# A gated mix of two attention layers: first phase and lead rearranged

## The chip, the cores and the metric

The kernel runs on one core of one Trainium2 chip. The core has five engines that work side by side, each through its own list of instructions in order: TensorE (PE; its weight loads are shown as PEld), VectorE (DVE), ScalarE (ACT), GpSimd (POOL) and SyncE (SP). An instruction waits on semaphores for the work it needs. Transfers between the core's memory (SBUF) and the device memory are issued from the lists of SP, ACT or POOL and carried out by 16 DMA engines. TensorE writes its results to PSUM, eight banks of 128 x 512 numbers, which ACT and DVE read.

The metric is the device time of one execution in microseconds (us), lower is better. The kernel before was run three times, and one execution was taken with the hardware profiler.

## The reference

Two attention layers with 32 heads of 18 dimensions work on the same input of 2048 rows by 576 columns, and a gate per row mixes their outputs. Layer A has its own keys and values per head; in layer B all heads share one key and one value. All is in 32-bit floating point.

```python
def reference(A_x, A_wqkv, A_wo, B_x, B_wq, B_wk, B_wv, B_wo, gate_w):
    ...
        qkv = (lambda x, *d: x.transpose(*d))((x @ wqkv).reshape(B, S, 3, H, Dh), 2, 0, 3, 1, 4)
        q, k, v = qkv[0], qkv[1], qkv[2]
        scale = Dh ** -0.5
        scores = jnp.einsum("bhqd,bhkd->bhqk", q, k) * scale
        p = _softmax(scores, axis=-1)
        o = jnp.einsum("bhqk,bhkd->bhqd", p, v)
        return (lambda x, *d: x.transpose(*d))(o, 0, 2, 1, 3).reshape(B, S, D) @ wo
    ...
        q = (lambda x, *d: x.transpose(*d))((x @ wq).reshape(B, S, H, Dh), 0, 2, 1, 3)
        k = x @ wk
        v = x @ wv
        scores = jnp.einsum("bhqd,bkd->bhqk", q, k) * (Dh ** -0.5)
    ...
    x = A_x
    g = _sigmoid((x * gate_w).sum(-1, keepdims=True))
    a = _A_ref(x, A_wqkv, A_wo)
    b = _B_ref(x, B_wq, B_wk, B_wv, B_wo)
    return g * a + (1 - g) * b
```

## The kernel before

The order of all engines' work is written out by hand: what stands first in the Python text stands first in each engine's list. TensorE multiplies in a reduced 32-bit format, so every operand of a product is kept as a high part and a low part (`h` and `l`, the remainder), and a product is the sum of high by high, high by low and low by high.

**First phase (L197 to L262).** The weights of all queries, shared key, shared value, gate and per-head keys lie side by side in `wall`, 14 row tiles of 128 columns (`MT`). `load5` (L120) brings five blocks of 128 contraction rows of a weight tile or an X tile with three transfers: one for four blocks and two for the last 64 rows, which are stored twice so that the fifth block carries both a high and a low part. X comes in eight tiles of 256 columns. `split_x` (L206) makes high and low parts of X: a copy on ACT, a subtract on DVE (L211) and a correction on DVE for the doubled rows (L212). `prep_w` (L134) does the same for a weight tile. `project(mt, c, w)` (L142) multiplies row tile `mt` by a chunk of 512 columns of X: 14 matmuls into one bank of the PSUM pool `ps` (three banks), then a copy of the high part by ACT (L150), the low part by DVE (L156), and a store of each: the high part from ACT's list into `qk_d[0]`, the low part from POOL's into `qk_d[1]`. Ten of the row tiles hold keys; there a difference of two chunks is stored in the same way (`kd_d`). Row tiles 0 and 1 are done together chunk by chunk while X arrives, the other twelve after that, four chunks each: 56 tiles of work in all. For chunk after chunk of row tile 0 the shared value is transposed by four small matmuls (`shared_v`, L174). At L236 to L240 and L253 the rows of the shared key and of the first three heads' queries are loaded back from the stored projections, from POOL's list. They are transfers of 18 rows of 2048 numbers; each goes twice into SBUF, to partitions from 0 (`SB`) and from 64 (`MB`).

Transfers are counted by sixteen semaphores in two rings of eight, one ring for SP and ACT together and one for POOL; a transfer is issued only when the one eight places before it in its ring has landed.

**Lead (T below 0 in the loop at L628).** Softmax needs the largest score of each row of a head before the exponentials. The step of maxima, `step_max(u, i, c)` (L329), multiplies 128 queries by 512 keys into a bank of the pool `pm` (four banks), and DVE takes the row maximum (L350). It runs `LEAD` = 22 steps of four banks ahead of the main loop. Before the loop proper, eleven rounds of two steps each (88 banks) are done as `LEADS` says, with `V` units between: `project_v` (L184), 32 units of 14 matmuls each that make layer A's values from X and are copied out by ACT (L190). `max_rows` (L352) sends a finished head's maxima through a small transfer into two extra rows of its queries.

**Main loop.** 512 rounds of two steps. A round has eight score matmuls (`s`, L376, into `ps`), each followed by an exponential on ACT (L383), the products with the values (`P`, `h`, `H`, L390), eight banks of maxima for later steps (`m`, and `x` with L344 and L347, which spare DVE one bank), and from some round on the output projection. In round T = 0 (`FIRST`) there are no products yet, and its eight banks of maxima stand between the scores.

Of the kernel before, what the change touches and what calls it, by code (L numbers as in the profile page):

```python
# [29 lines left out]
PROJ = [("h", "h", k, 128) for k in range(NKT)] + [("h", "l", k, 128) for k in range(NKT - 1)] + \  # L30
       [("l", "h", k, 128) for k in range(NKT)]
# [11 lines left out]
def gated_mix_kernel(ctx: ExitStack, tc: tile.TileContext, xT, wall, wv, wo, out):  # L43
# [15 lines left out]
    qk_d = [dram.tile([MT * P, S], F32, name=f"qk{x}") for x in "hl"]  # L59
    kd_d = [dram.tile([MT * P, 512], F32, name=f"kd{x}") for x in "hl"]  # L60
# [23 lines left out]
    dma(ones_r.rearrange("a (b c) -> (a b) c", c=32), ones)  # L84
# [5 lines left out]
    def load_rows(t, r, parts, eng=None):  # L90
        for b in (MB, SB):
            for i, y in enumerate(parts):
                dma(t[b + 18 * i:b + 18 * i + 18, :], qk_d[y][r:r + 18, :], eng)

    def load_q(u, eng=None):
        load_rows(qs[u % 3], q_row(u), (0, 0, 1), eng)

    def load_kd(t, r, eng=None):
        for i, y in enumerate((0, 1, 0)):
            dma(t[MB + 18 * i:MB + 18 * i + 18, :], kd_d[y][r:r + 18, :], eng)  # L100

    def load_k(t, r, eng=None):
        load_rows(t, r, (0, 1, 0), eng)
# [25 lines left out]
    def load_w(mt):  # L129
        st = wpool.tile([P, NKT, P], F32, name="wst", bufs=6)  # L130
        load5(st, wall[mt])
        return st

    def prep_w(st):  # L134
        w = {y: wpool.tile([P, NKT, P], F32R, name=f"w{y}") for y in "hl"}
        split_w(st, w, nc.vector)
        return w
# [4 lines left out]
    def project(mt, c, w):  # L142

        fp = ps_s.tile([P, 512], F32, name="ps")
        cs = slice(c * 512, (c + 1) * 512)
        for n, (a, b, k, kr) in enumerate(PROJ):
            nc.tensor.matmul(fp, w[a][:kr, k, :], X[b][:kr, k, cs], start=(n == 0), stop=(n == len(PROJ) - 1))  # L147
        h = stp.tile([P, 512], F32R, name="ph")
        l = stp.tile([P, 512], F32R, name="pl")
        nc.scalar.activation(h, fp, AF.Copy)  # L150
        if mt == 0 or c == 0 and mt in HAS_K:
            st = stp.tile([P, 512], F32, name="pst", bufs=3)
            nc.scalar.activation(st, fp, AF.Copy)
            if c == 0:
                KD[mt] = st
        nc.vector.tensor_tensor(l, fp, h.bitcast(F32), op=OP.subtract)  # L156
        if c == 1 and mt in HAS_K:
            d = stp.tile([P, 512], F32, name="pd", bufs=1)
            nc.vector.tensor_tensor(d, fp, KD.pop(mt), op=OP.subtract)
            dh, dl = (stp.tile([P, 512], F32R, name=f"pd{y}", bufs=1) for y in "hl")  # L160
            split(d, dh, dl, nc.scalar, nc.vector)
        dma(qk_d[0][mt * P:(mt + 1) * P, cs], h, nc.scalar)
        dma(qk_d[1][mt * P:(mt + 1) * P, cs], l, nc.gpsimd)
        if c == 1 and mt in HAS_K:
            dma(kd_d[0][mt * P:(mt + 1) * P, :], dh, nc.scalar)
            dma(kd_d[1][mt * P:(mt + 1) * P, :], dl, nc.gpsimd)
        if mt == 0:
            dma(z_d[cs], st[ROW_G:ROW_G + 1, :], nc.scalar)
            return c, st
# [11 lines left out]
    for t in vst:  # L181
        nc.gpsimd.memset(t, 1.0)
# [13 lines left out]

    WV = []  # L197
    with tc.tile_pool(name="xs", bufs=6, side="right") as xsp:
        W = [load_w(0)]
        XS = []  # L200

        def load_x(c):
            XS.append(xsp.tile([P, NKT, 256], F32, name="xs"))
            load5(XS[c], xT[:, 256 * c:256 * c + 256])

        def split_x(c):  # L206
            xs = XS[c]
            cs = slice(c * 256, (c + 1) * 256)
            xh = X["h"][:, :, cs]
            nc.scalar.activation(xh, xs, AF.Copy)  # L210
            nc.vector.tensor_tensor(X["l"][:, :, cs], xs[:, 0:4], xh[:, 0:4].bitcast(F32), op=OP.subtract)  # L211
            nc.vector.tensor_tensor(xh[64:128, 4], xs[64:128, 4], xh[64:128, 4].bitcast(F32), op=OP.subtract)  # L212

        for c in range(4):
            load_x(c)
        W.append(load_w(1))
        for c in range(4, 8):
            load_x(c)
        for mt in range(2, 6):
            W.append(load_w(mt))  # L220
        WP = [prep_w(W.pop(0))]
        for c in range(2):
            split_x(c)
# [9 lines left out]
    VS = [vwp.tile([P, NKT, 288], F32, name="vwst"), None]  # L233
    load5(VS[0], wv[:, 0:288])

    for b in (SB, MB):  # L236
        dma(ksb[b + 54:b + 56, :], ones_r, nc.gpsimd)
    load_k(ksb, ROW_KB, nc.gpsimd)
    load_kd(kdb, ROW_KB, nc.gpsimd)
    load_q(0, nc.gpsimd)  # L240

    def project_rest():
        WN = prep_w(W.pop(0))
        for mt in range(2, MT):
# [3 lines left out]
            if mt + 4 < MT:  # L248
                W.append(load_w(mt + 4))
            for c in range(4):  # L250
                project(mt, c, w)
            if mt in (4, 5):
                load_q(mt - 3, nc.gpsimd)  # L253
            if mt in (8, 11):
# [3 lines left out]
                if hf == 0:  # L258
                    VS[1] = vwp.tile([P, NKT, 288], F32, name="vwst")
                    load5(VS[1], wv[:, 288:576])  # L260

    project_rest()  # L262
# [66 lines left out]
    def step_max(u, i, c, low=False):  # L329
# [10 lines left out]
        pm = ps_m.tile([P, 512], F32, name="pm")  # L340
# [286 lines left out]
    LEADS = "V.A mA0 MA1 mA2 MA3 V.B mB0 MB1 mB2 MB3"  # L627
    for T in range(-LEAD, NSTEP + 2, 2):  # L628
        if T == 0:
            open_ph2()  # L630
# [3 lines left out]
        if M >= 16 and M % 16 == 0 and M // 16 - 1 < NU:  # L634
# [3 lines left out]
        for op in (LEADS if T < 0 else FIRST if T == 0 else ALONE if alone else UNIT if units else PLAIN).split():  # L638
            k, second, c = op[0], op[1:2] == "B", op[2:]
            if k == "V":  # L640
                while len(vunits) > 32 * (-T - 1 - (c == "B")) // LEAD:
                    project_v(*vunits[0], WV[vunits[0][1]])
                    vunits.pop(0)
            elif k == "x":
                if M + 2 < NSTEP:
                    step_max(*divmod(M + 2, 16), "x")
            elif k in "mM":
                step_max(*divmod(M + second, 16), int(c), k == "M")
# [56 lines left out]
```

## Time and profile before

| | us |
|---|---|
| runs of the kernel before | 2789.89, 2790.0, 2787.21 |
| median | 2789.89 |
| the profiled execution, its own time | 2789.11 |
| its span, first to last instruction | 2787.2 |
| TensorE busy | 2758.0 (99%) |
| VectorE busy | 2419.9 (87%) |
| ScalarE busy | 2433.3 (87%) |
| GpSimd busy | 211.9 (8%) |
| bytes moved | 214.53 MB, mean 77 GB/s |
| granted TensorE clock, mean | 0.997 |

Times in the rows below are from the start of the span. A row of the table of stretches gives, for each engine, its busy time and the number of its instructions, then the granted TensorE clock as a share of full speed, the mean busy share of the DMA engines and the bytes they moved a second. A row of the timeline gives start and duration, engine, line, operation, what it writes and reads, how often it came in a row, and in brackets how long the engine was idle before and what ended that. In a list of groups, the count is followed by the busy time, the mean of one in ns and the idle time before them. The chain that ended last is followed backwards from the last instruction, at each step to whatever released it. Instructions of one engine overlap a little, so a busy share of 100% does not say that the engine could not go faster. In a line that ends with three durations and a slash, these are the shortest, the median and the longest in ns, followed by the first and the last start.

### The profile page before, as it was taken

How to read it: one execution, taken by the hardware profiler on the slowest of the kernel's cores; microseconds unless marked ns; L12 is line 12 of the kernel's file. 1: busy time of each engine (PE TensorE's matmuls, PEld its weight loads, DVE VectorE, ACT ScalarE, POOL GpSimd, SP SyncE). 2: the span in 40 equal slices, each digit the busy share in tenths (PEclk: the TensorE clock that was granted, in tenths of full speed). 3: DMA queues.
4: the chain of work that ended last, by engine and by line, in shares of the span. 5: the costliest groups of instructions: out<-in, count | busy, mean ns of one | idle time of the engine just before them, and what ended most of it. 6: DMA issues, size and time to landing. Idle time of an engine off the chain costs nothing.

```text
span 2787.2 us, 57590 instructions
## 1 busy us (share of the span) xinstructions
PE 2758.0 (99%) x22132; PEld 1226.1 (44%) x22132; DVE 2419.9 (87%) x4495; ACT 2433.3 (87%) x4775; POOL 211.9 (8%) x368
## 2 busy tenths in 40 slices
PE   7999999999999999999999999999999999999998
PEld 5888433333333333333333444444434443334554
DVE  3346999999999999999999999999999999998873
ACT  3231899999999999999999999999999999998776
POOL 2220000001001100100110001000100010011000
PEclk9999999999999999999999999999999999999999
DMA  8662011111112111211143224222332223234412
GB/s 252 228 231 76 27 33 33 31 46 53 40 26 57 56 32 31 65 41 33 45 100 106 64 70 108 68 75 75 87 89 76 67 81 84 65 77 118 109 35 86
DMA packets 136738, 214.53 MB, mean 77 GB/s; under 512 B 55302, under 2 KB 94166, under 8 KB 124777
## 3 DMA queue, kind: packets, MB, share of 16 engines
q1 hardware_dynamic: 115751, 167.56, 23.0%
q10 hardware_dynamic: 14120, 22.30, 2.2%
q0 software_dynamic: 6592, 20.99, 2.2%
q8 instruction: 174, 2.85, 0.4%
q14 instruction: 101, 0.83, 0.1%
HBM read 137.23 MB, written 64.77 MB: 72 GB/s over the span
## 4 chain that ended last, share of the span: by engine, by line
PE 97%; DMA 2%; DVE 1%; SPq 0%; issue 0%; ACT 0%; POOL 0%; POOLq 0%; DVEq 0%
PE ps L376 41%; PE acc L390 38%; PE ps L147 5%; PE pm L341 5%; PE pm L516 4%; PE ps L187 2%; DMA qkl<-pl 0%; DMA ksb<-qkh 0%; DMA xs<-xT 0%; DMA wst<-wall 0%; SPq L49 0%; DVE mx L350 0%; PE pm L376 0%; DMA qkh<-ph 0%; DVE oacc L528 0%
## 5 line engine op out<-in xcount | busy, mean ns | idle before, releaser
L383 ACT ACTIVATE pt<-ps 128x512 f32<-128x512 f32 x4052 | 2127.4, 611 | 106.6 <-PE pm L341 42.8
L350 DVE TENSOR_REDUCE mx<-pm 128x1 f32<-128x512 f32 x3096 | 1976.3, 684 | 163.4 <-PE pm L341 121.3
L376 PE MATMUL ps<-qs,ksb 56*128 56x512 f32 x2688 | 907.9, 437 | 0.0
L341 PE MATMUL pm<-ksb,qs 54*128 54x512 f32 x2364 | 825.1, 445 | 0.9 <-DVE mx L350 0.3
L376 PEld LDWEIGHTS ps<-qs,ksb 56*128 56x128 f32 x2688 | 437.6, 184 | 683.9 <-ACT pt L383 660.4
L390 PE MATMUL acc<-pt,vb 128*19 128x256 f32 (+1 forms) x6144 | 592.4, 457 | 0.1
L390 PE MATMUL acc<-pt,vg 128*19 128x256 f32 (+1 forms) x5656 | 579.4, 481 | 0.4 <-DVE oe L402 0.4
L376 PE MATMUL ps<-qs,ksa 56*128 56x512 f32 x1364 | 456.3, 437 | 0.0
L341 PE MATMUL pm<-ksa,qs 54*128 54x512 f32 x1232 | 433.4, 443 | 0.0
L341 PEld LDWEIGHTS pm<-ksb,qs 54*128 54x128 f32 x2364 | 379.6, 184 | 10.5 <-DVE mx L350 4.0
L376 PEld LDWEIGHTS ps<-qs,ksa 56*128 56x128 f32 x1364 | 218.5, 184 | 343.9 <-ACT pt L383 317.0
L347 DVE CUSTOM_DVE_ANT_0 junk<-pm,xb 128x512 bf16<-128x512 f32 x500 | 340.1, 680 | 0.0
L344 ACT ACTIVATE xb<-pm 128x512 f32<-128x512 f32 x500 | 304.1, 608 | 0.0
L341 PEld LDWEIGHTS pm<-ksa,qs 54*128 54x128 f32 x1232 | 200.4, 184 | 0.9
L390 PEld LDWEIGHTS acc<-pt,vb 128*19 128x19 f32 x6144 | 104.2, 97 | 209.9 <-issue 199.6
L390 PEld LDWEIGHTS acc<-pt,vg 128*19 128x19 f32 x5656 | 96.5, 97 | 208.2 <-issue 195.4
L341 PE MATMUL pm<-kdb,qs 54*128 54x512 f32 x372 | 148.9, 400 | 0.0
L116 POOL CAST mh<-mt 128x32 fp32r<-128x32 f32 x64 | 13.5, 210 | 1712.2 <-DVE mt L358 1712.2
L156 DVE TENSOR_TENSOR pl<-ps,ph 128x512 fp32r<-128x512 f32 x56 | 38.5, 691 | 97.2 <-ACT ph L150 69.4
L150 ACT ACTIVATE ph<-ps 128x512 fp32r<-128x512 f32 x56 | 33.5, 597 | 101.6 <-PE ps L147 89.3
L147 PE MATMUL ps<-xh,wh 128*128 128x512 f32 x280 | 76.6, 405 | 19.2 <-ACT xh L210 13.1
L147 PE MATMUL ps<-xh,wl 128*128 128x512 f32 x280 | 72.7, 389 | 0.0
(103 smaller groups left out, 1316.4 us busy)
## 6 DMA issues: line engine op xcount, KB each, us to landing
qs<-qkh SPq DMA_DIRECT2D x244, 144.0 KB
qs<-qkl SPq DMA_DIRECT2D x122, 144.0 KB
qkh<-ph ACTq DMA_DIRECT2D x56, 256.0 KB
qkl<-pl POOLq DMA_DIRECT2D x56, 256.0 KB, 3.1
ksa<-qkh SPq DMA_DIRECT2D x88, 144.0 KB
onh<-oh SPq DMA_DIRECT2D x32, 256.0 KB
onl<-ol SPq DMA_DIRECT2D x32, 256.0 KB
oih<-onh SPq DMA_DIRECT2D x16, 512.0 KB
```

The source lines that it names most:

```text
L147: nc.tensor.matmul(fp, w[a][:kr, k, :], X[b][:kr, k, cs], start=(n == 0), stop=(n == len(PROJ) - 1))
L150: nc.scalar.activation(h, fp, AF.Copy)
L156: nc.vector.tensor_tensor(l, fp, h.bitcast(F32), op=OP.subtract)
L187: nc.tensor.matmul(fp[:, 0:288], X[b][:kr, k, st_ * P:(st_ + 1) * P], w[a][:kr, k, :], start=(n == 0), stop=(n == len(PROJ) - 1))
L341: nc.tensor.matmul(pm, qs[u % 3][b:b + 54, i * P:(i + 1) * P], k, start=True, stop=True)
L344: nc.scalar.activation(MX["x", u, i], pm, AF.Relu)
L347: nc.vector.tensor_tensor_reduce(junk, pm, MX.pop(("x", u, i)), 1.0, -3e38, op0=OP.add, op1=OP.max, accum_out=MX[u][:, i, c:c + 1])
L350: nc.vector.tensor_reduce(MX[u][:, i, c:c + 1], pm, axis=AX.X, op=OP.max)
L376: nc.tensor.matmul(ps, kst(u)[b:b + 56, i * P:(i + 1) * P], qs[u % 3][b:b + 56, c * 512:(c + 1) * 512], start=True, stop=True)
L383: nc.scalar.activation(pt, ps, AF.Exp, scale=SCALE)
L390: nc.tensor.matmul(acc[32 * j:32 * j + 19, a:b], v_of(u, i), PT[u, i, j][:, a:b], start=(i == 0), stop=(i == 15), skip_group_check=True)
L516: nc.tensor.matmul(fp[:, 0:288], o[b][:r, t, s2 * P:(s2 + 1) * P], w[a][:r, t, 288 * hf:288 * hf + 288], start=(n == 0), stop=(n == 3 * nt ...
```

## The change

It has several parts.

- The order of products in a tile (`PROJ`) puts the two of the fifth block last.
- The two DRAM tensors for high and low parts become one of twice the size, and `project` keeps both parts in one SBUF tile `phl` (four buffers instead of three and three) and stores them with one transfer from POOL's list; the same for `kd`. ACT issues no transfers in the first phase.
- `load5` takes four neighbouring rows to a partition instead of rows 128 apart; X comes as two tiles of 256 columns and three of 512. The 64-row rests of the first five tiles are issued from POOL. Three weight tiles come ahead of the later X tiles, and three row tiles are worked on per chunk. The very first tile is done in two halves of 256 columns.
- Six matmuls of constants run on TensorE before the first data. A copy of a constant is put at the head of ACT's list, and the store of that constant goes behind the loads.
- The row loads are collected and issued from SP's list, one after each tile of `project_rest`.
- The lead is written as 16 visits of two V units and six banks; of these, two banks go to the pool `ps` and four to `pm`. It does 24 steps, so round T = 0 has no maxima but `x`.

```diff
-PROJ = [("h", "h", k, 128) for k in range(NKT)] + [("h", "l", k, 128) for k in range(NKT - 1)] + \
-       [("l", "h", k, 128) for k in range(NKT)]
+PROJ = [(a, b, k, 128) for a, b in (("h", "h"), ("l", "h"), ("h", "l")) for k in range(NKT - 1)] + \
+       [("h", "h", NKT - 1, 128), ("l", "h", NKT - 1, 128)]
...
-    dma(ones_r.rearrange("a (b c) -> (a b) c", c=32), ones)
+    nc.scalar.activation(ones, ones, AF.Copy)
...
-    def load5(t, src):
-        dma(t[:, 0:4, :], src[0:512, :].rearrange("(k p) m -> p k m", p=P))
-        dma(t[0:64, 4, :], src[512:576, :])
-        dma(t[64:128, 4, :], src[512:576, :])
+    def load5(t, src, rest=None):
+        dma(t[:, 0:4, :], src[0:512, :].rearrange("(p k) m -> p k m", p=P))
+        dma(t[0:64, 4, :], src[512:576, :], rest)
+        dma(t[64:128, 4, :], src[512:576, :], rest)
...
-    def project(mt, c, w):
+    def project(mt, c, w, parts=1):
...
+        g = 512 // parts
+        for i in range(parts):
+            for n, (a, b, k, kr) in enumerate(PROJ):
+                nc.tensor.matmul(fp[:, g * i:g * i + g], w[a][:kr, k, :],
+                                 X[b][:kr, k, c * 512 + g * i:c * 512 + g * i + g],
+                                 start=(n == 0), stop=(n == len(PROJ) - 1))
+        hl = stp.tile([P, 2, 512], F32R, name="phl", bufs=4)
+        nc.scalar.activation(hl[:, 0, :], fp, AF.Copy)
...
+        nc.vector.tensor_tensor(hl[:, 1, :], fp, hl[:, 0, :].bitcast(F32), op=OP.subtract)
+        dma(qk_d[:, mt * P:(mt + 1) * P, cs].rearrange("a p f -> p a f"), hl, nc.gpsimd)
...
-        dma(qk_d[0][mt * P:(mt + 1) * P, cs], h, nc.scalar)
-        dma(qk_d[1][mt * P:(mt + 1) * P, cs], l, nc.gpsimd)
...
+    def later(o, i):
+        rows_back.append(lambda: dma(o, i))
+
+    def bring_row():
+        if rows_back:
+            rows_back.pop(0)()
...
+            XS.append(xsp.tile([P, NKT, 256 if half else 512], F32, name="xsh" if half else "xs", bufs=2))
+            load5(XS[c], xT[:, 256 * c:256 * c + 256] if half else xT[:, 512 * (c - 1):512 * c], rest)
...
+        W = [load_w(0, nc.gpsimd)]
+        load_x(0, nc.gpsimd)
+        load_x(1, nc.gpsimd)
+
+        warm = ps_m.tile([P, 512], F32, name="pm")
+        for i in range(6):
+            nc.tensor.matmul(warm[:, 0:304], ident, vb.rearrange("p k d -> p (k d)"), start=True, stop=True)
+        W.append(load_w(1, nc.gpsimd))
+        W.append(load_w(2, nc.gpsimd))
+        for c in range(2, 5):
             load_x(c)
+        dma(ones_r.rearrange("a (b c) -> (a b) c", c=32), ones)
+        for mt in range(3, 6):
             W.append(load_w(mt))
...
         for c in range(4):
+            keep = project(0, c, WP[0], 2 if c == 0 else 1)
+            if c == 3:
+                WN = prep_w(W.pop(0))
+            project(1, c, WP[1])
             if c < 3:
                 split_x(2 * c + 2)
                 split_x(2 * c + 3)
-            keep = project(0, c, WP[0])
-            project(1, c, WP[1])
             shared_v(*keep)
+            project(2, c, WP[2])
...
-    load_k(ksb, ROW_KB, nc.gpsimd)
-    load_kd(kdb, ROW_KB, nc.gpsimd)
-    load_q(0, nc.gpsimd)
+    load_k(ksb, ROW_KB, put=later)
+    load_kd(kdb, ROW_KB, put=later)
+    for u in range(3):
+        load_q(u, put=later)
...
             for c in range(4):
                 project(mt, c, w)
-            if mt in (4, 5):
-                load_q(mt - 3, nc.gpsimd)
+                bring_row()
...
+    banks = [(M, c) for M in range(LEAD + 2) for c in range(4)]
+    for v in range(16):
+        if v == 11:
+            max_rows(0)
+        for st_, hf in vunits[2 * v:2 * v + 2]:
+            project_v(st_, hf, WV[hf])
+        for n, (M, c) in enumerate(banks[6 * v:6 * v + 6]):
+            step_max(*divmod(M, 16), c, c % 2 == 1, ps_s if n < 2 else ps_m)
...
-    FIRST = "sA0 mA2 sA1 mA0 sA2 mA3 mA1 sA3 mB0 sB0 mB1 sB1 mB2 sB2 mB3 sB3 x"
+    FIRST = "sA0 sA1 sA2 sA3 sB0 sB1 sB2 sB3 x"
...
-    LEADS = "V.A mA0 MA1 mA2 MA3 V.B mB0 MB1 mB2 MB3"
-    for T in range(-LEAD, NSTEP + 2, 2):
+    for T in range(0, NSTEP + 2, 2):
```

More of the change, by code (lines that the diff above doesn't have):

```diff
@@ L56, in gated_mix_kernel @@
     ctx.enter_context(tc.manual_schedule())
-    qk_d = [dram.tile([MT * P, S], F32, name=f"qk{x}") for x in "hl"]
-    kd_d = [dram.tile([MT * P, 512], F32, name=f"kd{x}") for x in "hl"]
+    qk_d = dram.tile([2, MT * P, S], F32, name="qk")
+    kd_d = dram.tile([2, MT * P, 512], F32, name="kd")
     m_d = [dram.tile([P, 64], F32, name=f"m_d{i}") for i in range(4)]
@@ L127, in split_w, with load_w @@
         eng_l.tensor_tensor(w["l"], st, w["h"].bitcast(F32), op=OP.subtract)
-    def load_w(mt):
+    def load_w(mt, rest=None):
         st = wpool.tile([P, NKT, P], F32, name="wst", bufs=6)
-        load5(st, wall[mt])
+        load5(st, wall[mt], rest)
         return st
     def prep_w(st):
-        w = {y: wpool.tile([P, NKT, P], F32R, name=f"w{y}") for y in "hl"}
+        w = {y: wpool.tile([P, NKT, P], F32R, name=f"w{y}", bufs=3) for y in "hl"}
         split_w(st, w, nc.vector)
@@ L327, in gated_mix_kernel, with step_max @@
     MX = {}
-    def step_max(u, i, c, low=False):
+    def step_max(u, i, c, low=False, pool=ps_m):
         if u not in MX:
@@ L339, in step_max @@
             k = kst(u)[b:b + 54, c * 512:(c + 1) * 512]
-        pm = ps_m.tile([P, 512], F32, name="pm")
+        pm = pool.tile([P, 512], F32, name="pm" if pool is ps_m else "ps")
         nc.tensor.matmul(pm, qs[u % 3][b:b + 54, i * P:(i + 1) * P], k, start=True, stop=True)
```

104 lines of the change are left out of this document (47 added, 57 removed).

## The prediction, made before the changed kernel ran

> **What bounds the kernel now.** I read the engines' busy time by stage first, with edges where the work changes: the first matmul, the last long wait of the projections, the first gated V unit, the first score of the main loop, its second and third round.
>
> ```profile
> core 0: us, PE busy (x) PEld busy (x) DVE busy (x) ACT busy (x) POOL busy (x), PEclk, DMA share, GB/s
> 0.00:13.11 13.11, 0.00 (x0) 0.00 (x1) 3.33 (x7) 4.56 (x4) 1.57 (x9) 1.00 0.60 183
> 13.11:71.64 58.53, 50.80 (x212) 39.76 (x212) 23.91 (x36) 20.70 (x29) 15.24 (x29) 0.97 0.91 266
> 71.64:206.45 134.81, 134.81 (x587) 111.42 (x588) 52.32 (x73) 43.86 (x70) 34.60 (x65) 0.99 0.65 229
> 206.45:285.96 79.51, 79.51 (x538) 68.82 (x537) 53.47 (x89) 14.11 (x35) 1.93 (x11) 1.00 0.24 81
> 285.96:295.89 9.93, 8.98 (x33) 2.92 (x30) 9.07 (x16) 6.86 (x12) 0.00 (x0) 0.72 0.07 24
> 295.89:301.45 5.56, 5.56 (x44) 2.21 (x41) 4.27 (x8) 4.62 (x9) 0.00 (x0) 0.89 0.00 0
> ```
>
> TensorE sets the pace nearly everywhere. It stands still for 13.1 us at the start and for 58.53 - 50.80 = 7.7 us more up to 71.64; the first round of the loop (9.93 us) is the other weak place. The rounds from the second on keep their instructions in their order, so the change lives or dies in these 301 us.
>
> Next the longest pieces of the chain that ended last, which name the stalls and give the price of a tile (14 matmuls), and one group of the list of lines.
>
> ```profile
> 7.69 6.07 DMA xs<-xT
> 51.46 10.87 DMA ksb<-qkh
> 63.58 7.22 DMA qkl<-pl
> 71.64 135.20 PE ps L147 x588
> ...
> L174 PE MATMUL pm<-ident,pst 18*128 18x18 f32 x16 | 1.7, 215 | 1.6 <-ACT pst L153 1.6
> ```
>
> 135.20 / 588 = 0.230 us a matmul, 3.22 us a tile. The other 56 x 14 - 588 = 196 matmuls, 14 tiles, are done by 71.64. They need 45.1 us, and the 16 small transposes beside them 1.7, so the front loses 71.64 - 46.8 = 24.9 us: 13.1 before the first matmul, 7.7 idle, 4.1 in slow matmuls. That is the reserve of the first phase. The timeline shows where it goes.
>
> ```profile
> 1.01 0.29 POOL masks.py:199 TENSOR_SCALAR_AFFINE_SELECT ident<-ident 128x128 f32<-128x128 f32 x1
> 1.84 0.35 SPq L49 DMA_DIRECT2D ones_r<-ones  x1
> 2.24 1.74 SPq L49 DMA_DIRECT2D wst<-wall  x3
> 4.03 7.43 SPq L49 DMA_DIRECT2D xs<-xT  x12
> 5.85 1.28 ACT L126 ACT_TABLE_LOAD   x1 [5.85 <-DMA wst<-wall]
> 8.98 1.27 ACT L210 ACTIVATE xh<-xs 128x1280 fp32r<-128x1280 f32 x1 [1.10 <-DMA xs<-xT]
> 10.28 1.23 DVE L211 TENSOR_TENSOR xl<-xs,xh 128x1024 fp32r<-128x1024 f32 x1 [1.54 <-ACT xh L210]
> 11.54 0.42 DVE L212 TENSOR_TENSOR xh<-xs,xh 64x256 fp32r<-64x256 f32 x1
> 13.11 2.51 PE L147 MATMUL ps<-xh,wh 128*128 128x512 f32 x5 [13.11 <-ACT xh L210]
> 15.42 1.91 PE L147 MATMUL ps<-xl,wh 128*128 128x512 f32 x4
> 17.12 1.35 PE L147 MATMUL ps<-xh,wl 128*128 128x512 f32 x5
> 48.38 2.50 PE L147 MATMUL ps<-xh,wh 128*128 128x512 f32 x5 [3.37 <-ACT wh L126]
> 70.90 0.69 DVE L156 TENSOR_TENSOR pl<-ps,ph 128x512 fp32r<-128x512 f32 x1 [9.96 <-DMA qkl<-pl]
> ```
>
> Loads leave SP one by one (7.43 / 12 = 0.62 us each) behind a store that waits for DVE. The first tile needs two X tiles, and its first nine matmuls run at half speed (2.51 us for 5, later 1.35). At 70.90 DVE has waited 9.96 us for a store buffer, since the stores of the low part stand on POOL's queue behind the row loads of L237 to L240, and these in turn wait for other DMAs.
>
> **The change part by part.**
>
> *Start.* The constant's store leaves SP's head, so w0, X0, X1 can go from about 0.9, each as one issue; their 64-row rests go from POOL after 1.30.
>
> ```profile
> L49 POOL DMA_DIRECT2D qkl<-pl x56 | 30.6, 546 | 133.8 <-DVE pl L156 128.6 <-DMA wst<-wall 2.2 <-DVE vb L177 2.2
> qkl<-pl POOLq DMA_DIRECT2D x56, 256.0 KB, 3.1
> ```
>
> At 0.55 us an issue, X0's second rest (the fourth) leaves at 3.5. From issue to landing it takes between 1.9 us (before, w0: 3.98 to 5.85) and the median 3.1, so X0 is there at 5.4 to 6.6. The activation table is loaded meanwhile, by the copy on ones. Splitting X0 takes 1.27, and the two-part tile starts on 256 columns: first matmul at 6.7 to 7.9, taken 7.5. Its first hl product waits for xl (1.23 after xh), its k=4 pair for the correction (0.42); the second half's come another 1.65 later, so tile 0 ends near 11.1, 0.4 over its 3.22.
>
> *Idle matmuls.* They cost nothing by themselves: PE has no data until 7.5.
>
> ```profile
> 2763.79 1.19 PE L543 MATMUL pm<-vb,ident 128*128 128x304 f32 x4
> ```
>
> The same instruction starts every (1.19 - 0.42) / 3 = 0.26 us at full speed, 0.52 at half; six last 1.5 to 3.1 us from about 1.9 and end by 5, with 2.5 us of idle time behind. The slow start cost 2.51 + 1.91 - 9 x 0.23 = 2.3 us before. Nothing in this trace shows such a short burst; I take half of it, 1.0, bounds 0 and 2.3. The Trainium skill ("TensorE: Matmul & The Clock Gate", Part 1: The HAM clock gate) has full speed come after about 3.4 us of sustained matmuls and go after an idle window as long; the row agrees (slow from 13.11 to about 17.1, slow again after 3.37 us idle). By it, six idle matmuls fall just short, and this term would be 2.3, the sum below 1.3 smaller.
>
> *X and weights in order of need.* Three tiles a chunk ask 9.7 us of PE for 1.31 MB of X and 1.57 MB of stores.
>
> ```profile
> 10.00:20.00 10.00, 6.73 (x20) 4.91 (x21) 4.34 (x6) 3.67 (x5) 0.00 (x0) 1.00 1.00 283
> 30.00:40.00 10.00, 8.35 (x40) 6.48 (x39) 5.93 (x9) 4.80 (x7) 1.20 (x3) 1.00 0.92 303
> ```
>
> At 0.29 MB/us the second chunk (3.6 MB, with w0 to w2) lands near 16 and is split by 20; PE is through three tiles and transposes at 18.4. The third (6.5 MB with stores) lands near 25.5 for a split due at 25, the fourth has waited for the second's buffer and lands near 34 for one due at 35. PE and DMA are nearly even, so stalls are small but certain. Pieces of wall grow to 2 KB; I give no credit for it.
>
> *Stores and rows.* ACT sheds 70 issues; POOL issues 66 stores of 512 KB where it had 66 of 256 KB and 29 row loads. An issue costs between 0.55 (as now) and 1.09 (two of them): either hides under 3.22 a tile. Four buffers instead of three allow a store about 4 x 3.22 - 1.3 = 11.6 us before ACT's copy (0.6) or DVE's subtract (0.7) waits, and then, two tiles on, PE. The rows now stand on SP; behind a row that waits stand only weight loads, needed three row tiles (39 us) later. But SP runs ahead: some 15 rows follow within 45 to 60 us, together with stores. For late X and crowded stores I take 3.0 us of PE time, bounds 0 and 11 (the 7.22 and 3.37 us waits of before coming back). The transposes keep their 1.6 of idle time.
>
> Front after: 7.5 + 0.4 + 1.0 + 3.0 + 1.6 = 13.5 us lost, against 24.9. Gain 11.4; bounds 24.9 - (6.7 + 0.4 + 0 + 0 + 1.6) = 16.2 and 24.9 - (7.9 + 0.4 + 2.3 + 11 + 1.6) = 1.7. It shifts all that follows.
>
> *Lead.*
>
> ```profile
> 275.94 0.69 PEld L187 LDWEIGHTS ps<-vwh,xh 128*128 128x128 f32 x5 [0.25 <-ACT vst L190]
> 277.89 0.82 PE L187 MATMUL ps<-vwh,xh 128*128 128x288 f32 x5
> 279.82 0.73 PE L341 MATMUL pm<-ksb,qs 54*128 54x512 f32 x4
> 280.49 0.93 PE L187 MATMUL ps<-vwh,xh 128*128 128x288 f32 x5
> 282.55 0.84 PE L341 MATMUL pm<-ksb,qs 54*128 54x512 f32 x4
> 283.08 2.48 DVE L350 TENSOR_REDUCE mx<-pm 128x1 f32<-128x512 f32 x4 [0.24 <-PE pm L341]
> 283.32 0.93 PE L187 MATMUL ps<-vwh,xh 128*128 128x288 f32 x5
> ```
>
> Two V units take 279.82 - 275.94 = 3.88 us, four banks 0.67 (two by two on the halves of the array); where banks return after one unit, DVE (2.48 for four) isn't through and they cost 0.77. A visit of two units and six banks: 3.88 + 1.5 x 0.67 = 4.89; DVE needs 6 x 0.62 = 3.7 of it, and a bank's buffer (four of pm, one or two of ps) is written again only a visit later. Sixteen visits: 78.2 against 79.5, gain 1.3, with 8 banks more done. Bounds: 0.67 again for all six, 74.5, gain 5.0; or each visit 0.3 longer by waits for ps, which V units and banks now share, 83.0, loss 3.5.
>
> *First round.*
>
> ```profile
> L344 ACT ACTIVATE xb<-pm x41: 603/605/622, 313.7 to 498.8; 128x512 f32<-128x512 f32 x41
> 285.90 7.86 DVE L350 TENSOR_REDUCE mx<-pm 128x1 f32<-128x512 f32 x13 [0.33 <-PE pm L341]
> 290.00:295.89 5.89, 5.71 (x21) 1.81 (x19) 5.03 (x10) 4.07 (x8) 0.00 (x0) 0.52 0.01 3
> ```
>
> A steady round takes (498.8 - 313.7) / 40 = 4.63 us. Before, the first two take 9.93 + 5.56 = 15.5: DVE works off 13 banks, and the clock falls to 0.52. Without banks the first is ACT's nine instructions: 2 x 4.63 = 9.3, plus 1.0 for a clock that sags in the thin round too (0 to 2.8: the 5.89 us at 0.52 once more, 5.89 x 0.48). Gain 5.2, bounds 3.4 and 6.2.
>
> Sum: 11.4 + 1.3 + 5.2 = 17.9. The profiled execution took 2789.11 us (span 2787.2, 1.9 around it): 2771.2. The median of the runs is 0.8 higher; forecast **2772.0**.
>
> **The rivals.** (1) *DMA paces the front.* Up to 71.64 it moves 13.11 x 183 + 58.53 x 266 = 18.0 MB; if the 14th tile must still wait for as much, at 0.293 MB/us from 3 us on, that is 64.4: gain 7.2 in place of 11.4, 2776.2. For it: share 0.91 and 1.00. Against: these tiles need 15 MB by the shapes (X 5.2, nine weight tiles 3.0, the stores of ten tiles 5.2, ten rows 1.5).
>
> (2) *ps in the lead*: three ps buffers carry four tenants a visit, the 0.3 us of above, and gain -3.5: 2776.8. For it: PE waits for ACT's copy already (0.25 at 275.94). Against: each buffer has a unit's time, 1.9 us, to come free.
>
> (3) *Slower: stores fall behind throughout.* All stores now end in one queue. In the crowd a 256 KB store took 7.22 us; if one of 512 KB takes twice that, 14.4, the four buffers turn in (14.4 + 1.3) / 4 = 3.9 us, 0.7 over PE's 3.22, on some 53 tiles 37 us: 2772.0 + 37 - 3 = 2806. It decides from 13.4 us a store on (17.9 + 5.6 = 23.5 lost). Against: median landing 3.1, share 0.65 in the long stretch. Against this change speaks the Trainium skill ("SBUF — State Buffer", A bandwidth-pool intuition that's wrong): a DMA issued on POOL beside a DVE copy waits about 3.1 us for its descriptors. Five stores per four tiles in ten row tiles would then take 15.5 us where PE takes 12.9, 26 us later in all; this trace has 0.55 an issue beside DVE subtracts.
>
> (4) *It doesn't do what it says*: the idle matmuls don't hold the clock and the waits only move; inside the bounds of the front.
>
> **How the numbers follow.** Forecast 0.68, (1) 0.18, (2) 0.07, (3) 0.03, several mishaps together, between 2780 and 2795, 0.04. Range 2765 to 2780: below, a front gain of 16 with the lead's 1.3 and first rounds' 6.2 (2766) and a little of the lead's 5.0; above, (1) and (2) together. A change under 0.2%, 5.6 us, can't be told from none here: faster 0.93, same 0.04, slower 0.03.
>
> **What would show it.** First tile matmul near 7.5; three tiles by 18.5; the first V unit near 195 (206.45 before); no DVE wait for phl of several us. Sixteen lead visits of 4.9 us with no wait for ps; under 11 us from the first score to the third round. It is wrong if PE waits in long pieces for phl, for X, or for ps, or if the rounds after the third differ from 4.63.

## The result, and the profile after

| | before | after |
|---|---|---|
| median of the runs, us | 2789.27 (6 runs, 2787.21 to 2791.02) | 2769.27 (6 runs, 2768.61 to 2770.38) |
| ratio, 95% interval | | 0.9929 [0.9916, 0.9942] |
| span of the profiled execution, us | 2787.2 | 2767.8 |

The changed kernel is 20.0 us faster by the medians and 19.4 by the spans; 2772.0 was forecast, and 2769.27 lies in the range. The sum came out; several of its terms did not.

The busy time by stage in the changed kernel, with the columns and edges of the prediction's first table (only the edge after the projections' last long wait, which is gone, is now the start of the long stretch at 52.27):

```profile
core 0: us, PE busy (x) PEld busy (x) DVE busy (x) ACT busy (x) POOL busy (x), PEclk, DMA share, GB/s
0.00:12.72 12.72, 5.90 (x13) 3.76 (x13) 1.69 (x5) 3.57 (x5) 7.04 (x19) 0.92 0.82 240
12.72:52.27 39.55, 39.55 (x185) 32.70 (x185) 24.38 (x34) 18.84 (x26) 8.02 (x11) 0.94 0.73 243
52.27:194.93 142.66, 142.66 (x630) 118.09 (x631) 53.71 (x76) 45.51 (x75) 39.17 (x54) 1.00 0.71 252
194.93:271.67 76.74, 76.74 (x547) 67.73 (x545) 56.76 (x95) 14.08 (x35) 2.11 (x11) 1.00 0.26 87
271.67:278.65 6.98, 6.69 (x25) 1.93 (x22) 5.41 (x10) 6.19 (x12) 0.00 (x0) 0.87 0.10 34
278.65:283.89 5.24, 5.24 (x44) 2.02 (x40) 3.85 (x8) 4.14 (x9) 0.00 (x0) 0.85 0.00 0
```

From the first tile matmul to the end of the lead, TensorE's busy time equals the length of each stretch: the profile shows no wait of it there. The first V unit comes at 194.93 instead of 206.45 (gain 11.5), the lead takes 76.74 instead of 79.51 (2.8), the next two stretches 12.22 instead of 15.49 (3.3). That is 17.6. The steady loop gives 0.4 back: its last `xb` comes 17.2 us earlier, and so does the last run of DVE's output sums. Two rows of tile views show the first, before and after; two rows of DVE's timeline the second.

```profile
L344 ACT ACTIVATE xb<-pm x500: 597/605/631, 292.3 to 2705.9; 128x512 f32<-128x512 f32 x167
2777.58 3.65 DVE L528 TENSOR_TENSOR oacc<-pm,oacc 128x288 f32<-128x288 f32 x9 [0.34 <-PE pm L516]
```

```profile
L370 ACT ACTIVATE xb<-pm x500: 597/607/658, 276.2 to 2688.7; 128x512 f32<-128x512 f32 x167
2760.40 3.65 DVE L554 TENSOR_TENSOR oacc<-pm,oacc 128x288 f32<-128x288 f32 x9 [0.34 <-PE pm L542]
```

From there to the end before takes 2787.2 - 2777.58 = 9.6 and after 7.4: 2.2 us that no term of the sum foresaw. SP's waits in the last 50 us differ most in one row, first before, then after:

```profile
SPq L701 <- PEq L701: 2.6, 2, 2.1
```

```profile
SPq L736 <- PEq L736: 0.7, 2, 0.5
```

Before, SP waits 1.9 us longer for TensorE's sequencer (2.6 against 0.7 in all). What the sequencer did meanwhile the traces do not show: within the span, the last packet in a queue that fetches instructions starts 15.6 us before the end in the kernel before and 17.0 after, so a fetch of code does not tell the two apart. The cause stays open. All twelve kernels below, variants of the changed one, show an end of 7.1 to 8.1; for the kernel before there is one profile, and its six runs spread over 3.8 us, so the 2.2 may belong to that execution alone.

The start is where the forecast missed. The timeline of the first 19 us, with a row of the view of tile `xsh` (issues, and landing times in us):

```profile
1.92 5.90 PE L230 MATMUL pm<-vb,ident 128*128 128x304 f32 x12 [1.92 <-DVE ones L83]
2.73 2.06 POOL L49 DMA_DIRECT2D xsh<-xT  x4
3.73 6.22 SPq L49 DMA_DIRECT2D xs<-xT  x6
6.83 0.74 ACT L126 ACTIVATE wh<-wst 128x640 fp32r<-128x640 f32 x1 [4.57 <-DMA wst<-wall]
11.40 2.43 ACT L220 ACTIVATE xh<-xsh 128x1280 fp32r<-128x1280 f32 x2 [3.83 <-DMA xsh<-xT]
12.72 1.22 PE L150 MATMUL ps<-xh,wh 128*128 128x256 f32 x4 [4.90 <-ACT xh L220]
18.22 1.09 PE L150 MATMUL ps<-xh,wh 128*128 128x512 f32 x4
...
DMA to landing us min/median/max: 6.5/7.9/8.1
```

X0's rests leave POOL at 2.7 to 3.3, as forecast, but land only some 8 us later, and ACT's split waits for them until 11.40. The idle matmuls end at 7.82, TensorE stands 4.90 us, and the first tile then runs slowly: 18.22 - 12.72 = 5.50 us. Behind it there is nothing more to wait for, as the chain that ended last shows (start, length, what):

```profile
3.25 8.08 DMA xsh<-xT
12.72 8.86 PE ps L150 x42
...
52.27 143.05 PE ps L150 x630
```

630 matmuls in 143.05 us are 0.227 each, 3.18 a tile.

### The profile page after: what moved, and what is told of

The parts are those of the page before. It is cut to its first block, busy times and chain, and to the rows that moved or that the text cites. A ratio compares the mean times of both kernels' runs of the same rounds, so it can differ in the third digit from the quotient of the medians.

```text
span 2767.8 us, 57564 instructions
## 1 busy us (share of the span) xinstructions
PE 2755.4 (100%) x22158; PEld 1226.9 (44%) x22158; DVE 2420.0 (87%) x4495; ACT 2432.1 (88%) x4776; POOL 214.9 (8%) x349
## 4 chain that ended last, share of the span: by engine, by line
PE 99%; DVE 0%; DMA 0%; ACT 0%; POOL 0%; issue 0%; DVEq 0%; POOLq 0%; ACTq 0%
PE ps L402 42%; PE acc L416 39%; PE ps L150 7%; PE pm L367 5%; PE pm L542 4%; PE ps L186 2%; DMA xsh<-xT 0%; PE ps L367 0%; PE pm L402 0%; DVE mx L376 0%; DVE oacc L554 0%; PE pm L569 0%; PE ps L592 0%; ACT pt L409 0%; PE pm L175 0%
## 5 line engine op out<-in xcount | busy, mean ns | idle before, releaser
L367 PE MATMUL pm<-ksb,qs 54*128 54x512 f32 x2332 | 813.4, 443 | 0.0
L116 POOL CAST mh<-mt 128x32 fp32r<-128x32 f32 x64 | 13.4, 210 | 1696.0 <-DVE mt L384 1696.0
L154 ACT ACTIVATE phl<-ps 128x512 fp32r<-128x512 f32 x56 | 33.5, 597 | 104.4 <-PE ps L150 75.6
L160 DVE TENSOR_TENSOR phl<-ps,phl 128x512 fp32r<-128x512 f32 x56 | 38.7, 692 | 94.7 <-ACT phl L154 70.9
L150 PE MATMUL ps<-xh,wh 128*128 128x512 f32 (+1 forms) x285 | 83.7, 392 | 4.9 <-ACT xh L220 4.9
L150 PE MATMUL ps<-xh,wl 128*128 128x512 f32 (+1 forms) x285 | 82.9, 389 | 0.0
```

The source lines that it names most:

```text
L150: nc.tensor.matmul(fp[:, g * i:g * i + g], w[a][:kr, k, :], X[b][:kr, k, c * 512 + g * i:c * 512 + g * i + g], start=(n == 0), stop=(n == ...
L154: nc.scalar.activation(hl[:, 0, :], fp, AF.Copy)
L160: nc.vector.tensor_tensor(hl[:, 1, :], fp, hl[:, 0, :].bitcast(F32), op=OP.subtract)
L367: nc.tensor.matmul(pm, qs[u % 3][b:b + 54, i * P:(i + 1) * P], k, start=True, stop=True)
```

## The experiments

All are the changed kernel with one edit. Each was run once with its profile, except the last, which was timed in five rounds. "V" is the start of the first V unit's weights, 194.93 in the changed kernel; spans stand against its 2767.8. Two profiles of one kernel (`e1_rests_sp` and `e11_best`) differ by 1.1 us in span and 0.5 in V, so a difference of about 1 us between single runs shows little by itself.

**The rests on SP's list** (`e1_rests_sp`), then **on ACT's** (`e2_rests_act`):

```diff
-        W = [load_w(0, nc.gpsimd)]
-        load_x(0, nc.gpsimd)
-        load_x(1, nc.gpsimd)
+        W = [load_w(0)]
+        load_x(0)
+        load_x(1)
...
-        W.append(load_w(1, nc.gpsimd))
-        W.append(load_w(2, nc.gpsimd))
+        W.append(load_w(1))
+        W.append(load_w(2))
```

```diff
-        W = [load_w(0, nc.gpsimd)]
-        load_x(0, nc.gpsimd)
-        load_x(1, nc.gpsimd)
+        W = [load_w(0, nc.scalar)]
+        load_x(0, nc.scalar)
+        load_x(1, nc.scalar)
```

> The 64-row rests of w0, X0, X1, w1, w2 go back to SP's list; all else as changed. In the changed kernel X0's second rest was issued at 3.25 and landed 8.08 us later; its first matmul came at 12.72. Theory (turns): a small transfer in a ring of its own gets one turn for every long turn of the ring that carries the 256 to 1024 KB loads, so the rests land late although their own bytes are few. In SP's own ring, X0 is complete when the 0.98 MB up to it have moved: SP's sixth issue ends near 4.5, landing 6.5 to 7.5, first matmul 7.8 to 9, the first tile at full clock since the idle matmuls end at 7.8; the first V unit 3 to 5 us before the changed kernel's 195.3, span 2763 to 2765. Rival (bytes): the early loads share the DMA engines evenly whatever their ring, so X0 lands with X1, w1 and w2 near 11 in any case: first matmul at 12 to 13, span 2767 to 2769.

> The rests of w0, X0 and X1 are issued from ACT's list (a ring of its own, not POOL's); those of w1 and w2 stay on POOL. Theory (turns between rings): ACT's ring fares no better than POOL's; X0's rests land at 9 to 11, first matmul at 10.5 to 13. Rival (POOL's own way of issuing is slow to land): from ACT they land within 3 us of issue, at 6 to 7, first matmul 7.5 to 9, as with the rests on SP.

With the rests on SP, behind the tiles that they complete, the span is 2763.4 and V 190.56: 4.4 us better. Three rows of its timeline:

```profile
7.47 1.27 ACT L220 ACTIVATE xh<-xsh 128x1280 fp32r<-128x1280 f32 x1 [2.43 <-DMA xsh<-xT]
8.79 0.74 PE L150 MATMUL ps<-xh,wh 128*128 128x256 f32 x4 [1.94 <-ACT xh L220]
11.47 0.74 PE L150 MATMUL ps<-xh,wh 128*128 128x256 f32 x4 [0.44 <-ACT xh L220]
```

X0 is split at 7.47 instead of 11.40, although its rests now leave SP later than they left POOL. The tile runs at full speed at once (0.74 for four matmuls of 256 columns, not 1.22), after TensorE had stood only 1.94 us. With the rests on ACT the span is 2768.0 and nothing is gained; the timeline and the chain:

```profile
3.10 5.78 ACTq L49 DMA_DIRECT2D xsh<-xT  x4
11.64 1.22 PE L150 MATMUL ps<-xh,wh 128*128 128x256 f32 x4 [3.41 <-ACT xh L220]
```

```profile
1.93 6.46 DMA xsh<-xT
8.41 6.32 DMA xsh<-xT
```

X1's last rest left ACT at 8.41 and took 6.32 us, so the long landing isn't POOL's own: a small transfer from ACT's list, in a hardware queue of its own (q10, SP's is q1), meets it beside SP's large loads too. The Trainium skill ("DMA: Bandwidth & Descriptors", Queues, rings and completion order) has each DMA engine take the queues that have work in turn, a packet at a time, so that a packet of a rest waits behind one of a large load again and again; the 8.08 and 6.32 us agree with it, though the turns themselves are not in the trace. ACT's list was held by its own issues until 8.9 besides, so the 11.64 alone would not say it. What is shown is that issuing them from SP's list, in the order of need, cures most of it. In `e1_rests_sp` the later X tiles also leave SP later (from 10.2 instead of 3.73), and how much is owed to that and how much to the queues' turns was not separated.

**No idle matmuls** (`e3_no_idle`: the loop of six left out), **twelve of them** (`e4_idle12`), and **none with the rests on SP** (`e12_rests_sp_no_idle`):

```diff
-        for i in range(6):
+        for i in range(12):
```

> No idle matmuls; all else as changed. In the changed kernel they end at 7.82, 4.9 us before the first tile, which runs at a clock of 0.50 until about 16.7. Theory: they end too early to hold the clock and buy nothing: first matmul 12.5 to 12.9, first tile's 28 matmuls over 5.3 to 5.7 us again, first V unit within 0.4 us of 195.3, span 2767.3 to 2768.5. Rival: they shorten the slow stretch by part of a clock window even so: the first tile and its successor take 1 to 2 us more, span 2769 to 2770.

> Twelve idle matmuls instead of six. At the changed kernel's pace (six end at 7.82, the last at full clock or half) they end between 10.9 and 13.7. Theory (the clock is lost in the idle gap): the gap to the first matmul falls under 2 us, the first tile runs at full clock, about 3.7 us for its 28 matmuls instead of 5.5, and the first V unit comes 1.5 to 2 us earlier unless the idle ones themselves run past 12.7; span 2766 to 2767. Rival (the slow first tile is set by its operands, xl and the correction on DVE): first tile 5 us or more again, span within 0.5 of 2767.8.

> Rests on SP as in e1_rests_sp (first matmul 8.79, 1.9 us after the last idle one, first tile at clock 1.00, first V unit 190.56, span 2763.4), but no idle matmuls. Theory (idle matmuls pay only where the gap behind them is short): first matmul within 0.3 of 8.79, then half speed for 3 to 4 us, first V unit 1.3 to 2.2 later, span 2764.7 to 2765.8. Rival (the first tile waits for X1 anyway, so the clock costs nothing): within 0.5 of 2763.4.

Without them the span is 2767.0 and V 194.46, with twelve 2766.9 and 194.31: half a microsecond earlier, if anything. Twelve were expected to bring the tile to full speed, and did not:

```profile
1.92 8.26 PE L230 MATMUL pm<-vb,ident 128*128 128x304 f32 x24 [1.92 <-DVE ones L83]
12.74 1.22 PE L150 MATMUL ps<-xh,wh 128*128 128x256 f32 x4 [2.56 <-ACT xh L220]
```

They end at 10.18, and the tile 2.56 us later is slow again: that gap is enough for the clock to fall. By the Trainium skill ("TensorE: Matmul & The Clock Gate", Part 1: The HAM clock gate) one idle window of about 3.4 us brings the slow clock, and the windows run free of the kernel. Here a gap of 2.56 us sufficed, shorter than such a window, and one of 1.94 did not; the measurement decides. With the rests on SP, taking the idle matmuls out costs 0.5 us of span and 0.66 of V against `e1_rests_sp` (2763.9, 191.22), and 1.6 and 1.1 against the profile of the same kernel in `e11_best` (2762.3, 190.08): between what the theory and the rival expected.

```profile
8.92 1.22 PE L150 MATMUL ps<-xh,wh 128*128 128x256 f32 x4 [8.92 <-ACT xh L220]
```

The first tile is slow again. From its first matmul to the next tile's it takes 5.59 us against 4.76 in `e1_rests_sp`, which in turn waited 0.44 us for X1 within it. So the idle matmuls are worth some 0.5 to 1.6 us by these single runs, and only when X comes early.

**The row loads back on POOL's list** (`e5_rows_pool`):

```diff
-        rows_back.append(lambda: dma(o, i))
+        dma(o, i, nc.gpsimd)
...
-    for u in range(3):
-        load_q(u, put=later)
+    load_q(0, put=later)
...
+            if mt in (4, 5):
+                load_q(mt - 3, put=later)
```

> The row loads go back to POOL's list and to the places they had before (shared key and first query after the X phase, two more queries after row tiles 4 and 5); stores stay joined. In the changed kernel PE never waits between 12.7 and the first V unit at 194.9. Theory (order): before, the stalls came from stores that stood in POOL's list behind row loads which waited for their own data and their ring's places; now both parts of every tile would stand there, so PE waits again 3 to 10 us in pieces between 48 and 80, first V unit at 198 to 205, span 2771 to 2778. Rival (bytes): the stalls were bandwidth, which the shorter front no longer lacks: no PE wait above 0.5 us, first V unit within 1 us of 194.9, span 2767 to 2769.

The span is 2777.5 and V 204.31: 9.4 us of the front are lost. The timeline of POOL, ACT and TensorE tells how:

```profile
58.92 2.47 POOL L49 DMA_DIRECT2D ksb<-qk  x5
64.28 0.50 POOL L49 DMA_DIRECT2D ksb<-qk  x1 [2.89 <-DMA qk<-phl]
...
75.03 1.50 POOL L49 DMA_DIRECT2D qk<-phl  x2
...
83.66 0.60 ACT L154 ACTIVATE phl<-ps 128x512 fp32r<-128x512 f32 x1 [14.23 <-DMA qk<-phl]
85.04 2.07 PE L150 MATMUL ps<-xh,wh 128*128 128x512 f32 x4 [7.36 <-DVE phl L160]
```

From 58.9 to 75.0 POOL works off the rows, waiting for a DMA between them, and no store leaves. The four buffers are full by then: ACT's copy waits 14.23 us for a store to land, DVE's subtract waits for ACT, TensorE stands 7.36 us, and it starts again at the slow clock (2.07 for a run that takes 1.07). Together that is the 9.4.

**One store in place of two, undone** (`e6_two_stores`: the high part from ACT's list again, for `kd` too):

```diff
-        dma(qk_d[:, mt * P:(mt + 1) * P, cs].rearrange("a p f -> p a f"), hl, nc.gpsimd)
+        dma(qk_d[0, mt * P:(mt + 1) * P, cs], hl[:, 0, :], nc.scalar)
+        dma(qk_d[1, mt * P:(mt + 1) * P, cs], hl[:, 1, :], nc.gpsimd)
```

> Each tile's high part is stored from ACT's list and its low part from POOL's again; row loads stay on SP, four buffers stay. Theory (order): with the rows out of POOL's list two stores do no harm, and ACT has room for 66 issues of 0.33 us; PE waits under 1 us, first V unit within 1 us of 194.9, span 2767 to 2769. Rival (ring places): ACT's stores share eight places with SP's row and weight loads, so ACT waits for these, its copies come late and PE waits 2 to 6 us between 45 and 100, first V unit 197 to 201, span 2770 to 2774.

The span is 2768.6, V 196.19, 1.3 us later. ACT's waits in the first phase now have the first of these rows, TensorE's timeline the second:

```profile
ACT phl L154 <- DMA wst<-wall: 5.7, 2, 4.4
...
46.52 1.20 PE L150 MATMUL ps<-xh,wh 128*128 128x512 f32 x4 [0.93 <-ACT xh L222]
```

ACT shares a ring of eight transfers with SP, so its store waits for SP's weight loads to land, and what stands behind it on ACT's list waits too. After its first matmul TensorE waits 1.1 us in the front, 0.93 of them here, for ACT's split of the last chunk of X. That lies between the theory (under 1) and the rival (2 to 6).

**The third row tile after the X chunks** (`e10_two_tiles`):

```diff
             shared_v(*keep)
+        for c in range(4):
             project(2, c, WP[2])
```

> Two row tiles per chunk of X while X arrives, the third (row tile 2) afterwards; all else as changed. Theory: a chunk then asks 6.4 us of PE plus 0.8 for the transposes, while DMA needs 8 us at 0.29 MB/us for 1.31 MB of X and 1.05 MB of stores, and ACT and DVE 2.4 and 3.3 us for the split: PE waits 0.5 to 1.5 us at each of three chunks, first V unit 2 to 4 us later (197 to 199), span 2769.5 to 2772. Rival: X is there in time anyway, because the loads start earlier now; PE waits under 0.5 us in all and the first V unit stays within 0.5 us of 194.9.

The span is 2783.5 and V 210.01: 15.1 us, where the theory gave 2 to 4 and the rival 0.5. The view of stretches and TensorE's timeline:

```profile
20.00:30.00 10.00, 7.34 (x23) 5.54 (x22) 4.22 (x6) 2.91 (x3) 1.49 (x2) 0.67 0.46 161
...
24.33 2.08 PE L150 MATMUL ps<-xh,wh 128*128 128x512 f32 x4 [2.65 <-ACT xh L220]
36.74 1.84 PE L150 MATMUL ps<-xh,wh 128*128 128x512 f32 x4 [2.66 <-ACT xh L220]
48.02 2.07 PE L150 MATMUL ps<-xh,wh 128*128 128x512 f32 x4 [2.71 <-ACT xh L220]
```

The split of the next chunk stands behind tiles 0 and 1 on ACT's list, so without a third tile TensorE waits 2.7 us at each of three chunks, 8.0 in all, and each wait drops the clock for 4 to 6 us (2.08 for a run that takes 1.07 at full speed); that costs the other 7. The DMA is only 0.46 busy around the first of them, and all three splits follow ACT's copies without a wait for a transfer: X is there. The third tile covers the split and holds the clock. (Before, the split stood ahead of a chunk's tiles, so this kernel isn't before's order, and the 15.1 is the value of the cover in the new one.)

**The old lead and the old first round on the new front** (`e8_old_lead`: the rounds below T = 0 and `FIRST` as before), **the old first round alone** (`e9_first_banks`), and **all banks in one pool** (`e7_lead_pm`):

```diff
-    banks = [(M, c) for M in range(LEAD + 2) for c in range(4)]
+    banks = [(M, c) for M in range(LEAD) for c in range(4)]
...
-        for n, (M, c) in enumerate(banks[6 * v:6 * v + 6]):
+        for n, (M, c) in enumerate(banks[11 * v // 2:11 * (v + 1) // 2]):
...
-    FIRST = "sA0 sA1 sA2 sA3 sB0 sB1 sB2 sB3 x"
+    FIRST = "sA0 mA2 sA1 mA0 sA2 mA3 mA1 sA3 mB0 sB0 mB1 sB1 mB2 sB2 mB3 sB3 x"
```

```diff
-            step_max(*divmod(M, 16), c, c % 2 == 1, ps_s if n < 2 else ps_m)
+            step_max(*divmod(M, 16), c, c % 2 == 1, ps_m)
```

> First phase as changed, lead and first round as before (88 banks in eleven rounds, 8 banks in round T = 0). Theory (additive): the lead takes 79.5 us again where the changed one takes 76.7, and from the first score to the fourth score of the third round 15.5 us where the changed one takes 12.2; span 2.8 + 3.3 = 6.1 longer, 2773.9. Rival: part of the lead's gain comes from what the new front leaves behind (stores, buffers), so that the old lead takes 78 or less here; span 2772 or less.

> Sixteen visits carry 88 banks (five or six each) and round T = 0 its eight banks as before; all else as changed. From the first score to the fourth score of the third round the kernel before took 9.93 + 5.56 = 15.5 us, the changed one 12.2. Theory (DVE works off the eight banks while PE waits): 15 to 16 us again, the lead shorter by the eight banks' 4 x 0.22 to 0.3 = 0.9 to 1.2, span 2 to 2.8 longer, 2769.8 to 2770.6. Rival (the slow first round is the sagging clock, which stays): 12 to 13 us, span within 0.5 of 2767.8 or below.

> All six banks of a visit go to the pool pm (four buffers); all else as changed. The changed lead takes 76.5 us from its first V unit (194.93) to the first score's weights (271.44), 4.79 a visit. Theory (buffers): the fifth and sixth bank must wait until DVE has read the first and second of the same visit, 1.2 and 1.8 us after the first bank starts, so six banks take about 2.1 us instead of 0.9 and the visit 5.9 to 6.1: lead 94 to 97, span 2785 to 2789. Rival (DVE's own pace, 6 x 0.62 = 3.7 of a visit, leaves room): a visit stays under 5.2, lead under 83, span under 2775.

`e8_old_lead`: span 2773.3, 5.5 us slower, its lead 79.58; from its V (194.34) to the end it is 6.1 us longer, so lead and first rounds add up. `e9_first_banks`: 2770.4, 2.6 us slower, and 3.5 from V on, as its V came 0.9 earlier. Its lead, and from the first score to the fourth score of the second round:

```profile
194.01:270.77 76.76, 76.76 (x539) 67.82 (x537) 51.99 (x87) 14.10 (x35) 2.12 (x11) 1.00 0.25 88
270.77:281.69 10.92, 8.97 (x33) 2.92 (x31) 10.06 (x18) 6.84 (x12) 0.00 (x0) 0.73 0.06 22
```

The second stretch takes 6.98 in the changed kernel and 9.93 before. Eight banks fewer don't shorten the lead at all (76.74 with them): banks run in pairs, and of five the odd one takes a pair's time. So moving them out of the first round costs the lead nothing and brings 2.6 to 3.5 us. `e7_lead_pm`: span 2789.0, 21.2 us slower, its lead 99.5 (6.2 a visit). Its timeline:

```profile
204.35 3.68 DVE L376 TENSOR_REDUCE mx<-pm 128x1 f32<-128x512 f32 x6 [2.54 <-PE pm L367]
205.09 1.10 PE L367 MATMUL pm<-ksb,qs 54*128 54x512 f32 x2 [0.55 <-DVE mx L376]
```

With four buffers the fifth bank waits for DVE's first maximum and the sixth for its second, in every visit, while V units wait behind them. Two banks in `ps` are what lets a visit of six banks take 4.80 us.

**The better version** (`e11_best`): the kernel of `e1_rests_sp`, timed.

> The kernel of e1_rests_sp again, timed in rounds against the kernel before: rests of the first five tiles on SP, all else as changed. If the 4.4 us of its one look hold, its median is 2764.3 to 2766 where the changed kernel's is 2769.27, and the ratio to the kernel before 0.990 to 0.9925. If they were chance, it lies at 2768 to 2770.

Median 2764.43 us (five runs, 2764.07 to 2764.88) against 2789.83 for the kernel before on the same chip: ratio 0.9912 [0.9898, 0.9925], 4.8 us below the changed kernel's median. The changed kernel was timed on another occasion, against 2789.27 for the kernel before, but no run of one lies in the other's range.

## Why the prediction came out, step by step

*The reserve of the front* was 26.7 us, not 24.9: at 0.227 us a matmul, 784 matmuls and the transposes take 179.7, and 206.45 - 179.7 = 26.7. The stretch that gave 0.230 held a slow restart behind a wait:

```profile
71.64 2.37 PE L147 MATMUL ps<-xh,wh 128*128 128x512 f32 x5 [2.55 <-DVE pl L156]
```

*Start, failed.* The step was "From issue to landing it takes between 1.9 us (before, w0: 3.98 to 5.85) and the median 3.1, so X0 is there at 5.4 to 6.6". Both durations come from transfers that didn't stand beside several large loads in another ring; here it was 8. The first matmul came at 12.72, not 7.5, outside the bounds of 6.7 to 7.9. With the rests on SP's list, and the later loads behind them, it comes at 8.79 (`e1_rests_sp`, 4.4 us gained), so how the early loads are issued was the cause; 8.79 is still outside the bounds.

*Cold clock*: forecast 1.0 within 0 to 2.3. The first tile took 5.50 - 3.18 = 2.3 more, with the 0.4 of the two parts in it. The forecast's reason, a burst too short, was wrong. Six idle matmuls give twelve records in the trace, and the forecast had priced six: they lasted 5.90 us, not 1.5 to 3.1, and ended at 7.82, not by 5. That is long enough, also for the 3.4 us that the prediction held against it: in `e1_rests_sp` the tile behind the same six runs at full speed. What cost the clock was the gap of 4.90 us behind them, and `e4_idle12` shows that 2.56 is too long already.

*Stalls*: 3.0 forecast, none measured. The row loads were out of the stores' way; `e5_rows_pool` shows that this alone is worth 9.4. The late start is not the reason: in `e1_rests_sp`, which starts at 8.79, TensorE waits 0.44 us for X1 and for nothing else of that size up to V. *Transposes*: 1.6 forecast; with a third tile behind them, start and first tile leave only 194.93 - 179.7 - 12.72 - 2.3 = 0.2 for them and all else.

So the front's loss after was 15.2 instead of 13.5, out of a reserve of 26.7 instead of 24.9, and the gain of 11.5 agrees with the 11.4 by luck: the errors cancel. Of the 11.5 the start gave only 0.4 (12.72 for 13.11) and the waits that are gone 7.7; the rest is slow matmuls. With an earlier start the front does better: `e1_rests_sp` gains 15.9 there.

*Lead*: 76.74 / 16 = 4.80 a visit against 4.89; the six banks take 0.9, not 1.0, so the gain was 2.8, not 1.3. (The lower bound of 74.5 takes 0.77 us for the banks, not the 0.67 that it names, which gives 72.8; the forecast does not rest on it.) DVE's and the buffers' room was argued rightly, and `e7_lead_pm` shows what its lack costs.

*First rounds*: right in its value for after, wrong in the one for before. The step was "Before, the first two take 9.93 + 5.56 = 15.5". TensorE's timeline of before has the third round's first score, the seventeenth, here:

```profile
299.10 0.49 PE L376 MATMUL ps<-qs,ksb 56*128 56x512 f32 x1
...
301.45 0.50 PE L376 MATMUL ps<-qs,ksb 56*128 56x512 f32 x1
```

301.45 is its fourth, and 295.89 in the prediction's table the fourth of the second round. The two rounds took 299.10 - 285.96 = 13.1, and after they take 10.3, as forecast:

```profile
271.67 3.74 PE L402 MATMUL ps<-qs,ksb 56*128 56x512 f32 x8
...
282.01 0.49 PE L402 MATMUL ps<-qs,ksb 56*128 56x512 f32 x1
```

So 2.8 was to be had (3.3 up to the third round's fourth score), not 5.2; `e9_first_banks` gives 2.6 to 3.5 back. The clock sags in the thin round too, as forecast, but for half as long, first before, then after:

```profile
290.30:297.10 6.80, 6.71 (x25) 2.57 (x25) 5.07 (x10) 4.14 (x8) 0.00 (x0) 0.50 0.01 2
```

```profile
276.80:280.20 3.40, 3.40 (x16) 0.99 (x14) 1.99 (x5) 2.20 (x6) 0.00 (x0) 0.50 0.01 2
```

*The sum.* Lead and first rounds miss by 1.5 and 1.9 in opposite directions, and the steady loop and the end, which the sum left out, add 1.8. Measured: 11.5 + 2.8 + 3.3 - 0.4 + 2.2 = 19.4 of span, against 17.9. That the total came out is in good part luck.

*Rivals.* Transfers did not pace the front: TensorE waits for nothing from 12.72 on, and the DMA share is 0.73. The start did wait for one, the 8.08 us of X0's rest. The shared `ps` did not slow the lead; it carries it. Stores did not fall behind: they land after 4.1 us (median, at most 9.4), under the 13.4 from which it would have mattered, and POOL's issue takes 0.73 us where it took 0.55, well under a tile's 3.18. The change did what it says except for its idle matmuls, which did nothing here. Not undone one by one were the order of products, the layout of `load5`, the sizes of the X tiles and the two-part first tile, so what each of them is worth is open.

## What to carry to other kernels

Issue the transfers that complete a tile from the list of the large part and right behind it: a second list saves issue time and may cost many times that in landing. Give an engine whose result the next piece needs a whole piece of other work as cover, for a wait of 2.7 us was paid nearly twice in `e10_two_tiles`, once as idle time (8.0 us) and once in the clock (7). Read the edges of a stage by counting its instructions before subtracting stages, and check a sum term by term even when the total comes out.

## What the runs showed of the hardware

- Transfers of 64 KB issued from POOL landed after 6.5 to 8.1 us beside SP's large loads, and one from ACT after 6.32. In the first 13 us of the changed kernel POOL's queue moved 0.46 MB and SP's 2.69:

```profile
q1 hardware_dynamic: 1906, 2.69, 67.5%
q0 software_dynamic: 320, 0.46, 14.8%
```

- The clock fell to half after TensorE stood for 2.55 to 2.71 us, in five places of three kernels (before, `e4_idle12`, `e10_two_tiles`), not after 1.94 (`e1_rests_sp`), and the matmuls then ran at half speed for 3 to 6 us. It doesn't take a wait: in the first rounds of the main loop it fell too (0.50 from 290.3 before and from 276.8 after), with no wait of TensorE above 0.3 us in the 4 us before that.
- An issue from POOL took 0.52 us for the 64-row rests, 0.55 for stores of 128 rows and 0.73 for those of twice 128.
